# First pair of an attention-and-experts kernel: scores as three products, set-up work moved between engines and queues

## The chip, the cores and the metric

The kernel runs on one core of a Trainium2 chip. The metric is the time of one execution on the device in microseconds; less is better. Inputs and output are float32. Engines are named as in the profile: PE (TensorE matmul), PEld (its weight load), DVE (VectorE), ACT (ScalarE), POOL (GpSimd) and SP (SyncE, which only issues transfers).

## The reference, cut to what matters

Causal attention with a decay (4 batches, 8 heads, 576 positions, head dimension 64), then a routed expert layer, then a layer with a maximum of three products:

```python
scores = scale * np.matmul(q, k.transpose(0, 1, 3, 2))
cum = np.cumsum(np.log(np.clip(f, 0.0001, 1.0)), axis=-1)
scores = np.where(causal, -1e9, scores + cum[..., :, None] - cum[..., None, :])
attn = np.exp(scores - np.max(scores, axis=-1, keepdims=True))
attn = attn / (np.sum(attn, axis=-1, keepdims=True) + 1e-09)
x = np.matmul(attn, v)            # heads side by side: 2304 rows of 512
x = moe(x)                        # each row to one of 8 experts, two products
out = np.maximum(np.maximum(x @ w1, x @ w2), x @ w3) @ w_out
```

The softmax is the same when a constant is added to a row of scores, so only `-cum` of the key has to be added to the product, not that of the query.

## The kernel before, in words

**Pairs of heads.** The 32 heads are done as 16 pairs; a head's 576 queries are five tiles, taken in the order 4, 0, 3, 1, 2 (tile 0 of both heads is one product, done with the second head). For exactness each operand is split into a high part, rounded for the PE's `fp32r` mode, and a low part, the difference. Four tiles per pair, in three sets used in turn (pair `p` uses set `p % 3`): `At` holds the high part of q in its rows 0 to 63 and the low part in rows 64 to 127. `R1` holds the high part of k twice. `R2` holds the low part of k in rows 0 to 63 and, in rows 64 and 65, the decay `chi` and `clo` (high and low part of -8 times the cumulative sum). `Bt` holds the high part of q again in rows 0 to 63, copied out of `At` by a DMA, and ones in rows 64 and 65. A tile of scores is two products that accumulate in PSUM (line 377): `At` with `R1` over 128 rows, and `Bt` with `R2` over 66 rows (low k, and the decay through the ones). DVE then masks the tile and takes its maximum (line 400), ACT takes the exponential (line 424), PE transposes it (lines 439 to 447), ACT or DVE copies the transposed blocks to `PT`, PE multiplies them with V (line 506, one run of 32 products for a pair) and transposes the result back through `w144` (line 526).

**Set-up, in the order written (lines 282 to 313).** SP issues the loads of `f` and of pair 0 (q and k in halves, one half for each head). ACT's queue issues the loads of the experts' small inputs and of pair 1 (line 268). `decays` (line 74) clamps `f` (DVE), takes the logarithm (ACT), the running sum and its two parts (DVE). ACT rounds pair 0's halves to `At` and `R1` (line 297); SP copies each half of `At` to `Bt` (line 298) and brings the decay rows of pair 0 to `R2` (line 279). DVE makes the low parts of both halves (lines 303, 304). POOL fills at the very start the masks, `w144`, the ones of `Bt` in sets 1 and 2, the zero corners of the four `PT` and the last rows of the two V tiles. Then SP brings pair 1's decay rows and the first V.

**Planned part.** From line 314 on, a planner (`Sched`) writes the instructions: each task has an engine (or two to choose from), a cost, a priority and tasks it depends on; the planner keeps a modelled time per engine, starting at 9.0 for all, and always takes the task that can start first. What it fixes is each engine's order; on the chip the engines run those orders and wait for each other by semaphores. `split_tasks(p)` (line 326) makes the high parts of pair `p` on ACT or DVE, the copy to `Bt` on SP (line 349), and four low parts on POOL (lines 343, 346). `pair_out` (line 484) is the product with V and what follows. `late_rows` (line 95, the experts' normalised rows that go into `w144`) and `late_setup` (line 560) are chains of small tasks.

After attention, the experts' stage gathers rows and runs long streams of 384-column products on PE to the end.

Of the kernel before, what the change touches and what calls it, by code (L numbers as in the profile page):

```python
# [73 lines left out]
def decays(nc, g, sp):  # L74
    lf = g.lf
    chi = g.chi = sp.tile([B * H, S], F32R, name="chi")
    clo = g.clo = sp.tile([B * H, S], F32R, name="clo")
    nc.vector.tensor_scalar(out=lf, in0=lf, scalar1=1e-4, scalar2=1.0, op0=ALU.max, op1=ALU.min)
    nc.scalar.activation(out=lf, in_=lf, func=AF.Ln)
    cum = g.pp.tile([B * H, S], F32, tag="P", name="cum")  # L80
# [156 lines left out]
def attention(tc, g, qT, kT, v, x_dram, es):  # L237
# [22 lines left out]
    def zero_corners(i):  # L260
        d = PT[i][64:128, 0, 0:64]
        nc.gpsimd.memset(bass.AP(tensor=d.tensor, offset=d.offset, ap=[list(d.ap[0]), [S + 128, NBLK], [1, 64]]), 0.0)
# [14 lines left out]
    def load_decay(p):  # L277
        for r, c in enumerate((g.chi, g.clo)):
            nc.sync.dma_start(out=R2[p % NQ][64 + r:65 + r].bitcast(F32).rearrange("p r s -> p (r s)"),
                              in_=c[2 * p:2 * p + 2, :].bitcast(F32))  # L280
# [6 lines left out]
    for r in range(2):  # L287
        for t, src in ((q2, qT), (k2, kT)):
            nc.sync.dma_start(out=t[:, r], in_=src[0][:, r])
    g.mid_load()  # L290
    nc.vector.memset(g.nil, 0.0)
    nc.vector.memset(Bt[0][64:66].bitcast(F32), 1.0)
    g.decays()
    load_pair(1, nc.scalar)
    for r in range(2):
        for t, hi in ((q2, At[0]), (k2, R1[0])):
            nc.scalar.activation(out=hi[:, r], in_=t[:, r], func=AF.Copy)
        nc.sync.dma_start(out=Bt[0][0:64, r].bitcast(F32), in_=At[0][0:64, r].bitcast(F32))
        if r == 0:
            load_decay(0)  # L300
    nc.scalar.activation(out=g.nil[:, 1:2], in_=g.nil[:, 0:1], func=AF.Exp)
    for r in range(2):
        nc.vector.tensor_tensor(out=R2[0][0:64, r], in0=k2[0:64, r], in1=R1[0][0:64, r].bitcast(F32), op=ALU.subtract)
        nc.vector.tensor_tensor(out=At[0][64:128, r], in0=q2[64:128, r], in1=At[0][64:128, r].bitcast(F32), op=ALU.subtract)  # L304
    for i in range(1, NQ):
        nc.gpsimd.memset(Bt[i][64:66].bitcast(F32), 1.0)
    for i in range(NPT):
        zero_corners(i)
    for i in range(2):
        nc.gpsimd.memset(V[i][64:128, 4, :], 0.0)  # L310
# [1199 lines left out]
```

## Time and profile before

| what | us |
|---|---|
| median of 3 runs | 746.82 (745.94 to 749.03) |
| the profiled execution | 745.84 |
| its span in the trace | 744.1 |
| PE busy | 711.2 (96%) |
| DVE, ACT, POOL busy | 437.3, 375.2, 142.6 |

All times in the trace count from the start of the span. A row of the timeline gives an instruction's start, its duration, its engine and line, what it writes and reads, and in brackets how long the engine stood idle before it and what ended that. Matmuls overlap in the records, so the distance between two starts tells PE's pace, not the duration. The set-up and the first three pairs lie in the first 40 us, attention ends near 195 us, and the experts' stage fills the rest.

### The profile page before, as it was taken

To read this page: it belongs to the slowest core of one execution; us is meant where nothing else is said; L and a number is where in the kernel's file an instruction comes from. 1 tells how busy PE (TensorE), PEld (TensorE's weight loads), DVE (VectorE), ACT (ScalarE), POOL (GpSimd) and SP (SyncE) were. 2 spreads that over 40 slices of the span, in tenths; PEclk is the share of its full clock that TensorE was granted. 3 is DMA by queue.
4 is the path that set the end of the run, shared out by engine and by line. 5 is a ranking of instruction groups with operands and counts; after the bars stand their busy time and mean duration, and the time that the engine had idled before them with its cause. 6 is when DMAs were issued, how large, how long until landed. Compare 5 with 4: busy or idle time off the path is not lost. (4 is left out here: it accounts for less than half of the span.)

```text
span 744.1 us, 13151 instructions
## 1 busy us (share of the span) xinstructions
PE 711.2 (96%) x4814; PEld 671.4 (90%) x4814; DVE 437.3 (59%) x1118; ACT 375.2 (50%) x857; POOL 142.6 (19%) x140
## 2 busy tenths in 40 slices
PE   3999999999589999999999999999999999999996
PEld 2789888888489999999999999999899899998995
DVE  6788888878658887897687779512222123122220
ACT  5889899998348656546555654311211212112111
POOL 6658366440110310100210000010100100101001
PEclk9999999999869999999999999999999999999999
DMA  7768748521275665555667534000000100000001
GB/s 239 218 219 221 240 120 258 175 51 34 76 242 176 207 213 193 214 189 189 225 207 238 177 111 141 15 29 1 29 14 1 43 1 7 36 1 29 15 1 44
DMA packets 44708, 90.04 MB, mean 121 GB/s; under 512 B 23142, under 2 KB 23142, under 8 KB 44640
## 3 DMA queue, kind: packets, MB, share of 16 engines
q1 hardware_dynamic: 39984, 76.52, 32.6%
q0 software_dynamic: 3360, 9.74, 3.8%
q10 hardware_dynamic: 1296, 2.90, 1.1%
q8 instruction: 40, 0.66, 0.4%
q14 instruction: 28, 0.23, 0.1%
HBM read 74.83 MB, written 9.44 MB: 113 GB/s over the span
## 5 line engine op out<-in xcount | busy, mean ns | idle before, releaser
L1289 DVE TENSOR_TENSOR tm<-pm,tm 128x384 f32<-128x384 f32 x72 | 40.1, 557 | 178.9 <-PE pm L959 178.8
L958 PE MATMUL pm<-x_y,m 128*128 128x384 f32 x432 | 144.4, 334 | 0.0
L959 PE MATMUL pm<-x_y,m 128*128 128x384 f32 x432 | 144.4, 334 | 0.0
L957 PE MATMUL pm<-x_y,m 128*128 128x384 f32 x432 | 144.4, 334 | 0.0
L1003 DVE TENSOR_TENSOR w<-stg,w 128x1024 fp32r<-128x1024 f32 x64 | 78.0, 1223 | 22.6 <-ACT w L986 21.9
L986 ACT ACTIVATE w<-stg 128x1024 fp32r<-128x1024 f32 x62 | 65.2, 1056 | 42.4 <-DMA stg<-in_w_dram 25.7
L424 ACT ACTIVATE P<-P,nm 128x576 f32<-128x576 f32 (+2 forms) x144 | 83.8, 586 | 4.8 <-DVE nm L400 4.5
L1324 POOL DMA_INDIRECT out_dram<-oo,ctidx x18 | 17.8, 987 | 332.8 <-ACT oo L1321 329.7
L958 PEld LDWEIGHTS pm<-x_y,m 128*128 128x128 f32 x432 | 81.1, 188 | 0.3
L957 PEld LDWEIGHTS pm<-x_y,m 128*128 128x128 f32 x432 | 81.1, 188 | 0.2
L959 PEld LDWEIGHTS pm<-x_y,m 128*128 128x128 f32 x432 | 81.1, 188 | 0.0
L957 PE MATMUL ph<-x,w 128*128 128x384 f32 (+7 forms) x256 | 78.9, 308 | 0.7 <-ACT x L986 0.7
L958 PE MATMUL ph<-x,w 128*128 128x384 f32 (+7 forms) x256 | 78.8, 308 | 0.4 <-DVE novi L843 0.4
L957 PE MATMUL py<-h,w 128*128 128x384 f32 (+7 forms) x256 | 78.7, 307 | 0.0
L959 PE MATMUL ph<-x,w 128*128 128x384 f32 (+7 forms) x256 | 78.5, 307 | 0.0
L958 PE MATMUL py<-h,w 128*128 128x384 f32 (+7 forms) x256 | 77.4, 303 | 0.0
L959 PE MATMUL py<-h,w 128*128 128x384 f32 (+7 forms) x256 | 77.4, 302 | 0.0
L986 ACT ACTIVATE g<-tm 128x384 fp32r<-128x384 f32 x36 | 18.9, 524 | 111.0 <-DVE tm L1289 111.0
L377 PE MATMUL s<-R,At 128*128 128x288 f32 (+3 forms) x160 | 60.7, 384 | 9.4 <-DVE At L304 8.2
L1113 POOL DMA_INDIRECT gat<-x_dram,gidx x23 | 27.9, 1212 | 199.6 <-PE xt L1120 156.4
L400 DVE CUSTOM_DVE_ANT_0 P<-s,mask 128x288 f32<-128x288 f32 (+3 forms) x128 | 58.3, 475 | 7.7 <-PE s L377 7.0
L443 PE MATMUL t<-ident,P 128*128 128x128 f32 x320 | 57.0, 278 | 0.0
(256 smaller groups left out, 1533.3 us busy)
## 6 DMA issues: line engine op xcount, KB each, us to landing
stg<-in_w_dram SPq DMA_DIRECT2D x61, 512.0 KB
sd<-in_m_dram SPq DMA_DIRECT2D x18, 512.0 KB
q<-in_q_dram SPq DMA_DIRECT2D x14, 576.0 KB
k<-in_k_dram SPq DMA_DIRECT2D x14, 576.0 KB
Bt<-At SPq DMA_DIRECT2D x15, 288.0 KB
V<-in_v_dram SPq DMA_DIRECT2D x4, 1024.0 KB
x_dram<-XL SPq DMA_DIRECT2D x62, 64.0 KB
sd_o<-in_mo_dram SPq DMA_DIRECT2D x6, 512.0 KB
```

The lines of the kernel that those rows point to most:

```text
L377: nc.tensor.matmul(st[:, 0:wp], lt[0:kk, r, q0:q0 + 128], rt[0:kk, r, j0:j0 + wp], start=(ps_i == 0), stop=(ps_i == 1))
L400: nc.vector.tensor_tensor_reduce(out=P[0:n, j0:j0 + w], in0=st_.pop((h, t, k))[0:n, 0:w], in1=g.mask[0:n, m0:m0 + w], scale=-0.125, scalar ...
L424: nc.scalar.activation(out=P[0:n, 0:ext], in_=P[0:n, 0:ext], func=AF.Exp, bias=nm[0:n, k:k + 1], scale=-1.0, accum_out=sums[b][0:n, t, c:c ...
L443: nc.tensor.transpose(w[:, 128 * a:128 * a + 128], P[:, 128 * a:128 * a + 128], g.ident)
L957: nc.tensor.matmul(out, whi, xhi, start=start, stop=False)
L958: nc.tensor.matmul(out, whi, xlo, start=False, stop=False)
L959: nc.tensor.matmul(out, wlo, xhi, start=False, stop=stop)
L986: nc.scalar.activation(out=out, in_=in_, func=AF.Copy)
L1003: ENG[e].tensor_tensor(out=w[:, 1], in0=t, in1=w[:, 0].bitcast(F32), op=ALU.subtract)
L1113: nc.gpsimd.indirect_dma_start(out=t[0:n], out_offset=None, in_=x_dram, in_offset=bass.IndirectOffsetOnAxis(ap=idx, axis=0))
L1289: nc.vector.tensor_tensor(out=mx[0], in0=mx["p", w][:, 0:MC], in1=mx[0], op=ALU.max)
L1324: nc.gpsimd.indirect_dma_start(out=out, out_offset=bass.IndirectOffsetOnAxis(ap=g.sidx[:, col:col + 1], axis=0), in_=o[1], in_offset=None, ...
```

## The change

For pair 0 the second product takes q's high part straight from `At` (rows 0 to 63) and only low k from `R2` (64 rows); a third product adds the decay: `pick`, a tile of 64 rows in which rows r and 32+r are ones for head r and the others zero, against `cc`, which holds `chi` of all 32 heads in rows 0 to 31 and `clo` in rows 32 to 63. So pair 0 needs neither copies to `Bt` nor decay rows in `R2`. `pick` is made by POOL (a fill and two selects) and rounded by ACT. Pair 1's loads go to SP's queue right behind those of pair 0; pair 2's loads depend on pair 1's high q. The low parts of head 1 are made by POOL, those of head 0 stay on DVE. DVE gets some fills of POOL (ones of `Bt` in set 1, last rows of V 0, corners of two `PT`); POOL's other fills and `w144` become planned tasks behind the low parts of pair 1, with the experts' rows behind `w144`. `hold` is a write of the same column of `nil` by DVE and then by POOL, which makes POOL wait until DVE has come that far; it stands after the clamp and after DVE's low parts. The dummy exponential that loads ACT's table moves ahead of the last rounding. The planner's clocks start at 8.2 (PE, DVE), 8.4 (ACT) and 11.0 (POOL). The load of the second V waits for the first pair's product with V.

```diff
--- before.py
+++ after.py
@@ -71,12 +71,29 @@
                             pattern=[[0, NPAIR], [-64, 2], [-1, D]], channel_multiplier=1)
 
 
-def decays(nc, g, sp):
+def pick_rows(nc, g, sp):
+    pick = g.ones_at = sp.tile([2 * B * H, 2, 128], F32, name="ones_at")
+    g.pick = sp.tile([2 * B * H, 2, 128], F32R, name="pick")
+    nc.gpsimd.memset(pick, 0.0)
+    for c in range(2):
+        nc.gpsimd.affine_select(out=pick, in_=pick, compare_op=ALU.not_equal, fill=1.0, base=-B * H * c,
+                                pattern=[[-1, 2], [0, 128]], channel_multiplier=1)
+
+
+def hold(nc, g):
+    nc.vector.memset(g.nil[:, 2:3], 0.0)
+    nc.gpsimd.memset(g.nil[:, 2:3], 0.0)
+
+
+def decays(nc, g, sp, meanwhile):
     lf = g.lf
-    chi = g.chi = sp.tile([B * H, S], F32R, name="chi")
-    clo = g.clo = sp.tile([B * H, S], F32R, name="clo")
+    g.cc = sp.tile([2 * B * H, S], F32R, name="cc")
+    chi, clo = g.cc[0:B * H], g.cc[B * H:]
     nc.vector.tensor_scalar(out=lf, in0=lf, scalar1=1e-4, scalar2=1.0, op0=ALU.max, op1=ALU.min)
+    hold(nc, g)
+    meanwhile()
     nc.scalar.activation(out=lf, in_=lf, func=AF.Ln)
+    nc.scalar.activation(out=g.pick, in_=g.ones_at, func=AF.Copy)
     cum = g.pp.tile([B * H, S], F32, tag="P", name="cum")
     nc.vector.tensor_tensor_scan(out=cum, data0=lf, data1=g.nil[0:B * H, 0:1].to_broadcast([B * H, S]), initial=0.0,
                                  op0=ALU.add, op1=ALU.add)
@@ -257,9 +274,9 @@
     V = [fx.tile([128, NBLK, H * D], F32, name=f"V{i}") for i in range(2)]
     vt, raws, sums, XL, Pt, st_, tl_ = {}, {}, {}, {}, {}, {}, {}
 
-    def zero_corners(i):
+    def zero_corners(i, e=nc.gpsimd):
         d = PT[i][64:128, 0, 0:64]
-        nc.gpsimd.memset(bass.AP(tensor=d.tensor, offset=d.offset, ap=[list(d.ap[0]), [S + 128, NBLK], [1, 64]]), 0.0)
+        e.memset(bass.AP(tensor=d.tensor, offset=d.offset, ap=[list(d.ap[0]), [S + 128, NBLK], [1, 64]]), 0.0)
 
     def load_pair(p, eng=None):
         q2 = ld.tile([128, 2, S], F32, tag="q2", name=f"q2_{p}")
@@ -275,9 +292,10 @@
         vt[b] = t
 
     def load_decay(p):
-        for r, c in enumerate((g.chi, g.clo)):
+        for r in range(2):
+            h = B * H * r + 2 * p
             nc.sync.dma_start(out=R2[p % NQ][64 + r:65 + r].bitcast(F32).rearrange("p r s -> p (r s)"),
-                              in_=c[2 * p:2 * p + 2, :].bitcast(F32))
+                              in_=g.cc[h:h + 2, :].bitcast(F32))
 
     g.lf = pp.tile([B * H, S], F32, tag="P", name="lf")
     nc.sync.dma_start(out=g.lf, in_=g.f_in)
@@ -287,31 +305,29 @@
     for r in range(2):
         for t, src in ((q2, qT), (k2, kT)):
             nc.sync.dma_start(out=t[:, r], in_=src[0][:, r])
+    load_pair(1)
     g.mid_load()
     nc.vector.memset(g.nil, 0.0)
-    nc.vector.memset(Bt[0][64:66].bitcast(F32), 1.0)
-    g.decays()
-    load_pair(1, nc.scalar)
+    nc.vector.memset(Bt[1][64:66].bitcast(F32), 1.0)
+    nc.vector.memset(V[0][64:128, 4, :], 0.0)
+    g.decays(lambda: [zero_corners(i, nc.vector) for i in range(2)])
+    low_q = lambda e, r: e.tensor_tensor(out=At[0][64:128, r], in0=q2[64:128, r], in1=At[0][64:128, r].bitcast(F32), op=ALU.subtract)
+    low_k = lambda e, r: e.tensor_tensor(out=R2[0][0:64, r], in0=k2[0:64, r], in1=R1[0][0:64, r].bitcast(F32), op=ALU.subtract)
     for r in range(2):
-        for t, hi in ((q2, At[0]), (k2, R1[0])):
-            nc.scalar.activation(out=hi[:, r], in_=t[:, r], func=AF.Copy)
-        nc.sync.dma_start(out=Bt[0][0:64, r].bitcast(F32), in_=At[0][0:64, r].bitcast(F32))
-        if r == 0:
-            load_decay(0)
-    nc.scalar.activation(out=g.nil[:, 1:2], in_=g.nil[:, 0:1], func=AF.Exp)
-    for r in range(2):
-        nc.vector.tensor_tensor(out=R2[0][0:64, r], in0=k2[0:64, r], in1=R1[0][0:64, r].bitcast(F32), op=ALU.subtract)
-        nc.vector.tensor_tensor(out=At[0][64:128, r], in0=q2[64:128, r], in1=At[0][64:128, r].bitcast(F32), op=ALU.subtract)
-    for i in range(1, NQ):
-        nc.gpsimd.memset(Bt[i][64:66].bitcast(F32), 1.0)
-    for i in range(NPT):
-        zero_corners(i)
-    for i in range(2):
-        nc.gpsimd.memset(V[i][64:128, 4, :], 0.0)
+        nc.scalar.activation(out=At[0][:, r], in_=q2[:, r], func=AF.Copy)
+        if r == 1:
+            nc.scalar.activation(out=g.nil[:, 1:2], in_=g.nil[:, 0:1], func=AF.Exp)
+        nc.scalar.activation(out=R1[0][:, r], in_=k2[:, r], func=AF.Copy)
+    low_k(nc.vector, 0)
+    low_q(nc.vector, 0)
+    hold(nc, g)
+    low_q(nc.gpsimd, 1)
+    low_k(nc.gpsimd, 1)
     load_decay(1)
     load_v(0)
 
     sd = Sched({"s": 3, "P": NPB, "t": 2, "tl": 1, "o": 2, "ot": 2}, 9.0)
+    sd.clk.update(PE=8.2, DVE=8.2, Pool=11.0, ACT=8.4)
     act = lambda n: 0.06 + n / 1200
     dve = lambda n: 0.07 + n / 960
     pe = lambda n: 0.02 + n / 2400
@@ -321,14 +337,28 @@
     slot = {(h, t): 5 * h + i for h in range(NH) for i, t in enumerate(order)}
     side, ready, fs, fr, fe, ft, fv, ftv, fo, fb, fn_ = {}, {0: []}, {}, {}, {}, {}, {}, {}, {}, {}, {}
     vdep = {0: None}
-    rows_done = sd.chain(g.late_rows(), 8)
+
+    def fill_corners():
+        zero_corners(2)
+        zero_corners(3)
+
+    def fills():
+        late = lambda cost, prio, fn, i: sd.task("Pool", cost, lambda e: fn(), prio, ready[i])
+        late(1.0, 8, lambda: nc.gpsimd.memset(Bt[2][64:66].bitcast(F32), 1.0), 1)
+        vdep["pt"] = late(0.7, 9, fill_corners, 1)
+        base = late(1.5, 12, g.w144_base, 1)
+        vdep[1] = late(0.5, 30, lambda: nc.gpsimd.memset(V[1][64:128, 4, :], 0.0), 2)
+        late(1.05, 20, lambda: nc.gpsimd.memset(Bt[0][64:66].bitcast(F32), 1.0), 2)
+        return base
+
 
     def split_tasks(p):
         i, u = p % NQ, 10 * p - 6
-        load = None
+        load = Task(("SP",), 0.0, None, 0, [], (), 0.0)
+        load.end, load.by = 9.0, "SP"
         if p > 1:
             old = [fs[h, t, k] for h in (2 * p - 6, 2 * p - 5) for t in range(NBLK) for k in range(1 + (t == 4))] if p >= NQ else []
-            load = sd.task("SP", 0.9, lambda e: load_pair(p), u - 8, ready[p - 2], lat=4.5)
+            load = sd.task("SP", 0.9, lambda e: load_pair(p), u - 8, ready[p - 2] + ([ready[1][0]] if p == 2 else []), lat=4.5)
             dec = sd.task("SP", 1.3, lambda e: load_decay(p), u - 4, old, lat=2.0)
         else:
             old, dec = [], None
@@ -367,15 +397,20 @@
         def fn(e):
             st = st_[h, t, k] = ps_s.tile([128, 512], F32, tag="s", name=f"s_{h}_{t}_{k}")
             wp = max(w, 192)
-            for ps_i, (lt, rt, kk) in enumerate(((At[i], R1[i], 128), (Bt[i], R2[i], 66))):
+            for ps_i, (lt, rt, kk) in enumerate(((At[i], R1[i], 128), (Bt[i] if p else At[i], R2[i], 66 if p else 64))):
                 if t == 0:
                     nc.tensor.matmul(st[:, 0:192].rearrange("p (r j) -> p r j", r=2), lt[0:kk].rearrange("p r q -> p (r q)")[:, S - 64:S + 64],
                                      rt[0:kk, :, 0:96],
-                                     start=(ps_i == 0), stop=(ps_i == 1))
+                                     start=(ps_i == 0), stop=(p > 0 and ps_i == 1))
                     continue
                 q0 = ROW0[t] - (0 if r else 64)
                 nc.tensor.matmul(st[:, 0:wp], lt[0:kk, r, q0:q0 + 128],
-                                 rt[0:kk, r, j0:j0 + wp], start=(ps_i == 0), stop=(ps_i == 1))
+                                 rt[0:kk, r, j0:j0 + wp], start=(ps_i == 0), stop=(p > 0 and ps_i == 1))
+            if p == 0 and t == 0:
+                for x in range(2):
+                    nc.tensor.matmul(st[:, 96 * x:96 * x + 96], g.pick[:, x], g.cc[:, 0:96], start=False, stop=(x == 1))
+            elif p == 0:
+                nc.tensor.matmul(st[:, 0:wp], g.pick[:, r], g.cc[:, j0:j0 + wp], start=False, stop=True)
 
         fs[h, t, k] = sd.task("PE", pe(2 * max(w, 192)), fn, slot[h, t] - LEAD, side.get(h, []), get=("s", (h, t, k)))
 
@@ -507,7 +542,7 @@
                                          vt[b][:, a, (2 * hp + r) * D:(2 * hp + r + 1) * D],
                                          PT[(2 * p + r) % NPT][:, a, lo:c0 + w], start=(a == 0), stop=(a == na - 1))
 
-        fo[p] = sd.task("PE", 2.85, pv, u0 + 1, [fv[h, t] for h in hs for t in order] + [vdep[b]],
+        fo[p] = sd.task("PE", 2.85, pv, u0 + 1, [fv[h, t] for h in hs for t in order] + [vdep[b], vdep["pt"] if p == 1 else None],
                         get=[("o", ("po", p, u)) for u in range(2)], kind="tile")
         for u, (c0, w) in enumerate(RNG):
             o = {}
@@ -555,13 +590,16 @@
 
     last = [None]
     split_tasks(1)
-    consts_done = sd.chain(g.late_setup(), 25, ready[1])
+    split_tasks(2)
+    base = fills()
+    rows_done = sd.chain(g.late_rows(), 12, [base])
+    consts_done = sd.chain(g.late_setup(), 25, [base])
     for p in range(NP):
         b, hp = divmod(p, NPAIR)
-        if p + 2 < NP:
+        if 0 < p < NP - 2:
             split_tasks(p + 2)
         if hp == 1 and b + 1 < B:
-            vdep[b + 1] = sd.task("SP", 3.3, lambda e, b=b: load_v(b + 1), 40 * b + 20, [fo[NPAIR * b - 1]] if b else [], lat=2.0)
+            vdep[b + 1] = sd.task("SP", 3.3, lambda e, b=b: load_v(b + 1), 40 * b + 20, [fo[NPAIR * b - 1] if b else fo[0]], lat=2.0)
         head(2 * p)
         head(2 * p + 1)
         pair_out(p)
@@ -1453,12 +1491,12 @@
             g.qk = ea.enter_context(tc.tile_pool(name="qk", bufs=1))
             sp = ea.enter_context(tc.tile_pool(name="sp", bufs=1))
             consts(nc, g, cp, sp)
-            w144_base(nc, g, sp)
-            pair_mask(nc, g, sp)
-            g.nil = sp.tile([128, 2], F32, name="nil")
+            pick_rows(nc, g, sp)
+            g.nil = sp.tile([128, 3], F32, name="nil")
             g.f_in = f
             g.mid_load = lambda: expert_load(nc, g, emb, tau, sp)
-            g.decays = lambda: decays(nc, g, sp)
+            g.decays = lambda zeros: decays(nc, g, sp, lambda: (pair_mask(nc, g, sp), zeros()))
+            g.w144_base = lambda: w144_base(nc, g, sp)
             g.late_rows = lambda: expert_rows(nc, g, sp, g.ps_o)
             g.late_setup = lambda: routing_consts(nc, g, cp)
             g.batch_done = lambda b, X: route_batch(nc, g, b, X, rp, g.ps_o)
```

## Rows read from the trace of the kernel before

**Rows 1.** The page: its first line and PE's share of the span.

```profile
span 744.1 us, 13151 instructions
...
PE 711.2 (96%) x4814; PEld 671.4 (90%) x4814; DVE 437.3 (59%) x1118; ACT 375.2 (50%) x857; POOL 142.6 (19%) x140
```

**Rows 2.** Windows: stretch, length, busy us (instructions) per engine, PEclk, DMA share, GB/s.

```profile
0.00:10.00 10.00, 0.58 (x1) 0.29 (x1) 5.49 (x8) 4.02 (x5) 9.04 (x21) 1.00 0.76 250
...
20.00:24.00 4.00, 3.07 (x17) 2.75 (x17) 1.77 (x8) 2.00 (x7) 3.72 (x18) 1.00 1.03 309
...
40.00:60.00 20.00, 20.00 (x176) 17.27 (x176) 17.59 (x69) 17.64 (x53) 12.03 (x9) 1.00 0.68 200
...
215.00:220.00 5.00, 5.00 (x27) 5.00 (x26) 2.34 (x3) 2.35 (x3) 0.00 (x0) 0.87 0.97 339
```

**Rows 3.** PE's waits from 0 to 60 us: us in total, times, longest.

```profile
PE s L377 <- DMA Bt<-At: 4.3, 2, 3.4
...
PE pe L116 <- DVE emb L112: 0.7, 1, 0.7
```

**Rows 4.** Timeline of PE: first scores, the pace's rise, begin of the experts' stage.

```profile
8.22 0.58 PE L377 MATMUL s<-R,At 128*128 128x288 f32 x1 [8.22 <-DVE At L304]
...
12.20 0.61 PE L377 MATMUL s<-R,Bt 66*128 66x288 f32 x1 [3.40 <-DMA Bt<-At]
...
12.61 0.44 PE L377 MATMUL s<-R,At 128*128 128x288 f32 x1
...
12.85 0.44 PE L377 MATMUL s<-R,Bt 66*128 66x288 f32 x1
...
14.95 0.53 PE L377 MATMUL s<-R,At 128*128 128x192 f32 x1 [0.91 <-DVE nm L400]
...
21.74 0.30 PE L377 MATMUL s<-R,At 128*128 128x288 f32 x1
22.97 0.40 PE L377 MATMUL s<-R,Bt 66*128 66x288 f32 x1 [0.93 <-DMA Bt<-At]
23.21 0.30 PE L377 MATMUL s<-R,At 128*128 128x288 f32 x1
23.35 0.30 PE L377 MATMUL s<-R,Bt 66*128 66x288 f32 x1
...
205.11 2.34 PE L1120 MATMUL xt<-ident,gat 128*128 128x128 f32 x8 [4.07 <-DMA gat<-x_dram,gidx]
```

**Rows 5.** Timeline of the issuing queues (SPq, ACTq) in the set-up.

```profile
3.31 0.36 ACTq L268 DMA_DIRECT2D q<-in_q_dram  x1
...
4.97 0.57 SPq L298 DMA_DIRECT2D Bt<-At  x1
...
11.83 0.40 SPq L273 DMA_DIRECT2D V<-in_v_dram  x1
...
14.42 0.54 SPq L349 DMA_DIRECT2D Bt<-At  x1
```

**Rows 6.** Timeline of ACT and DVE: pair 0's high and low parts.

```profile
4.26 0.68 ACT L297 ACTIVATE At<-q 128x576 fp32r<-128x576 f32 x1 [0.28 <-DMA q<-in_q_dram]
...
7.32 0.76 DVE L304 TENSOR_TENSOR At<-q,At 64x576 fp32r<-64x576 f32 x1
...
7.96 0.69 ACT L297 ACTIVATE At<-q 128x576 fp32r<-128x576 f32 x1 [2.31 <-DMA q<-in_q_dram]
...
11.23 0.68 ACT L297 ACTIVATE R<-k 128x576 fp32r<-128x576 f32 x1 [2.58 <-DMA k<-in_k_dram]
```

**Rows 7.** Groups by line and shape, 0 to 32 us: busy us, mean ns.

```profile
L343 POOL TENSOR_TENSOR At<-q,At 64x576 fp32r<-64x576 f32 x3 | 4.2, 1411 | 0.2
...
L306 POOL MEMSET Bt<- 2x1152 f32 x2 | 2.3, 1180 | 0.0
...
L400 DVE CUSTOM_DVE_ANT_0 P<-s,mask 128x448 f32<-128x448 f32 x3 | 1.9, 617 | 1.3 <-PE s L377 1.3
...
L262 POOL MEMSET PT<- 64x320 f32 x4 | 1.3, 358 | 0.0
```

## The prediction, made before the change was run

> **What bounds the kernel now.** I read the page's first lines, then the windows, then PE's waits, then the timelines of the first 24 us. PE is busy 711.2 of 744.1 us [rows 1], and from 40 to 60 us it has no idle time at all [rows 2]: once PE has its first scores, its stream sets the end, and what is saved in front of that stream is saved at the end. So the place to look at is the set-up, where PE does 0.58 us of work in the first 10 us [rows 2]. PE's first product starts at 8.22, when DVE has the low part of q. The second one waits 3.40 us more, to 12.20, for the copy of q to `Bt` by DMA [rows 4]. That copy was issued at 4.97 [rows 5]; it had no work to do but moving 144 KB, on engines that were 0.76 busy in this stretch at 250 GB/s [rows 2]. PE waits twice for such a copy, 4.3 us in all [rows 3]; the second wait is pair 1's, 0.93 us before 22.97 [rows 4], for a copy issued at 14.42 behind V and pair 2's loads [rows 5].
>
> The pace matters too. [...] In the experts' stage PE starts at 205.11 [rows 4], and a mean of 0.87 in 215 to 220 [rows 2] puts the rise 3.7 us before 220, at 216.3: 11.2 us after the start. For the changed start I take 9.5 us, with 6.8 and 11.2 as ends.
>
> **The change, part by part.** *The start.* Head 0's three products need high q and k (ACT), both low parts (DVE) and `cc` (DVE), all done before the low q that ends at 7.32 + 0.76 = 8.1 [rows 6]. So PE goes on from its first product at 8.2 instead of 12.2. New in front of that: `pick` on POOL, a fill and two selects. Between a fill of 358 ns and one of 1180 ns each [rows 7] that is 1.1 to 3.5 us on an engine that has two masks ahead of it; I take 1.2, done near 3.5. ACT rounds it in at most the 0.68 us of a larger rounding [rows 6] before it takes q at 4.26, where it stood 0.28 us idle [rows 6]. At the low end nothing moves, at the high end the start moves 2 us; I take 0. DVE's new fills (0.36 each for two corners [rows 7], some 0.5 for V) lie in front of the clamp and beside ACT's logarithm; without that cover they would cost their 1.2 us.
>
> *The third product.* [...] The second product costs the same over 64 rows as over 66.
>
> *Adding up to the point where pair 1 begins.* Before, PE ran from 12.20 to 21.7 with one wait of 0.9 us (14.95, behind DVE's rounding of pair 1's q): 8.6 us at half pace, worth 4.3 at full. Afterwards the same work is 4.3 + 1.36 = 5.7, less the first product. From 8.2 at half pace until 17.7 PE does 4.75 of it, and the last 0.8 to 0.9 at full pace: it is there at 18.5 instead of 21.7, a gain of 3.2. With the rise at 15.0 it is there at 17.1 (4.6), at 19.4 there is no rest left (2.3).
>
> *Pair 1's wait.* Its copy to `Bt` was issued at 14.42 and landed at 22.97. Now its high q is made from loads that finish near 11 us (below), the copy is issued some 4 us earlier, and pair 2's loads stand behind it, not ahead. Needed at 18.5, behind V's 1 MB and itself: 11 + 1.3 MB at 250 GB/s = 16 to 17. So the 0.93 us go. Sum: 3.2 + 0.93 = 4.1 us. Bounds 2.3 + 0.9 = 3.2 and 4.6 + 0.9 = 5.5.
>
> *Queues.* SP loses two copies to `Bt` and two decay rows of pair 0, and gains pair 1's two loads, in front of pair 1's decay rows and V; ACT's queue loses them. Nothing of pair 0 waits behind them on SP any more. In the trace of before, pair 0's second half of q lets ACT start only at 7.96 and that of k at 11.23, after waits of 2.31 and 2.58 us [rows 6], while pair 1's loads, issued from ACT at 3.31 [rows 5], move over the same engines. Put behind them on one queue, pair 0's 1.25 MB at 250 GB/s should be there near 7 and pair 1's near 11. [...]
>
> *Head 1's low parts on POOL.* 1.41 us each against DVE's 0.76 [rows 6, 7]. They are queued behind the second `hold`, at 8.1: 8.1 + 1.41, then 1.41 behind k's rounding, with gaps 11.0 to 11.2. PE needs them after head 0's 1536 x 3 columns at half pace, 8.2 + 3.84 = 12.0. So nothing on the path; the slack is 0.8 to 1.0. What waits behind them on POOL are pair 1's four low parts: they start behind the rounding of pair 1's k, near 13, and at 1.41 with gaps of 0.1 the first two are done at 16, where PE needs them by 18.5, the others at 19. The first `hold` stops POOL until the clamp is over; behind it stands only the pair mask, which no tile needs before the second head.
>
> *Late fills and the experts' rows.* `Bt`'s ones 1.18, two corners 0.72 [rows 7] and `w144`, priced by the largest row at 1.2 to 2.4, now follow pair 1's low parts: POOL is free for pair 2 near 23, and two low parts for its first head take 3. Sixteen pairs end near 195 us, some 10 us each, so PE needs them about 10 us after 18.5: they are hidden, by 2 to 3 us. The chain of the experts' rows starts later, and PE, which waited 0.7 us for it [rows 3], may wait as long again or not at all; I leave it as it is, plus or minus 0.7. *Planner clocks* change only orders. DVE needs 0.62 us for a tile of 448 columns [rows 7], whose three products take PE 1.1 at half pace, so masking keeps up unless it stands behind a rounding that waits for data.
>
> **The number.** 745.84 (the profiled execution, span 744.1 and 1.7 around it) - 4.1 = 741.7. That execution lies 1.0 below the median of 746.82 and inside the range of the runs; for a median I say 742.0. About 0.5%, 3.7 us, is what a measurement here can tell from no change.
>
> **Rivals.**
> *The stall moves to pair 1* (chance 0.13). PE comes to pair 1 earlier, and its low parts (POOL until 16 for the first two) or its `Bt` copy are late. For it: the copy took 8.5 us from issue to use [rows 4, 5], and POOL has 2.8 us more ahead of pair 1. If pair 1's second product still starts at 22.97, the whole gain is gone: 745.8, the same. Against it: what stood ahead of that copy, pair 2's loads, is now behind it.
> *The queue doesn't order* (0.12). Then the change of queues doesn't do what it says, and pair 0's second half of k still lands at 11.2. ACT, in order, stands until 11.9; POOL's low k is done at 13.3 and PE waits 1.3 us for head 1, and ACT's first exponentials come 1 us later still: about 743.8, the same. For it: 16 engines at 0.76 whoever issues. Against it: the first halves, alone on the queue, were there at 4.26.
> *PE stays at half pace* (0.07, slower). Place: the first three heads. PE runs early but in pieces, waiting on POOL, on roundings in front of masks and on exponentials, and its pace rises only after a run without breaks. Each us at half pace costs 0.5. From a rise at 17.7 the 4.1 us are used up when the pace rises after 26; at 30 the time is 747.9, past 33 it is over 0.5% slower. For it: 11.2 us in the experts' stage, after a start in pieces. Against it: with three score buffers and 0.62 us per mask, head 0 gives an unbroken 3.8 us, and head 1 follows.
>
> **How the numbers follow.** The forecast has 0.68: of its 3.2 to 5.5 us, some 0.48 lies above 3.7 and 0.20 below. The two rivals that give most of it back add 0.25 to the same, of which I move 0.02 to faster for a part of the stall only. The slow one gives 0.05 slower and 0.02 the same. Faster 0.50, same 0.45, slower 0.05. The range starts at 742.0 - 2.7 = 739.3: the high gain, 5.5, with PE's 0.7 us of waiting gone as well, both counted against 4.1, is 2.1, and 0.6 for the spread of the runs below their median. It ends at 746.2, which takes in the moved stall at 745.8 and leaves out the slow case.
>
> **What would show it.** Right: PE's second and third products at 8.4 to 8.8 with no wait for a DMA; 11 more matmul groups on line 377 and its neighbours; ACT's second roundings near 6 and 8.5; POOL's head 1 low parts at 8.2 to 11.2; the 0.14 us pace by 17.7; pair 1's scores from 18.5 without a wait; and everything from 40 us on the same, some 4 us earlier, down to PE's first work in the experts' stage, near 201 in place of 205.11. Wrong: a wait of PE at pair 1 or for line 346 of over 1 us; ACT idle until 11; or an earlier start whose lead is smaller at 60 us than at 20, which would mean that DVE and ACT, each at 88% in 40 to 60 us [rows 2], set that stretch and not PE.

## The result and the profile after

The changed kernel takes **755.16 us**, median of 4 runs (753.97 to 755.58), against 747.15 (745.94 to 749.03) for the kernel before on the same chip: ratio 1.0102, 95% interval 1.0078 to 1.0127. It is slower by 1%; 742.0 was forecast. The profiled execution took 755.44 with a span of 753.7, against 745.84 and 744.1.

The first lines of the page of the kernel after:

```profile
span 753.7 us, 13179 instructions
...
PE 721.9 (96%) x4826; PEld 678.2 (90%) x4826; DVE 445.0 (59%) x1123; ACT 373.1 (49%) x856; POOL 144.7 (19%) x144
```

PE's share is what it was [rows 1], but it is busy 10.7 us longer (721.9 against 711.2). So PE lost little to waiting; its own work takes longer. Its waits in the first 60 us, kernel after (idle us, how often, longest):

```profile
PE s L407 <- DVE nil L84: 8.6, 1, 8.6
...
PE pe L133 <- DVE emb L129: 2.0, 1, 2.0
```

Both waits for `Bt` [rows 3] are gone, and PE starts at 8.6, 0.4 us behind the 8.2 that was forecast. A wait of 2.0 us for the experts' rows stands in the place of one of 0.7 [rows 3]. Timeline of PE, kernel after (a row with x2 holds a tile's first two products and shows the shape of the first):

```profile
8.58 1.11 PE L407 MATMUL s<-R,At 128*128 128x288 f32 x2 [8.58 <-DVE nil L84]
9.49 0.44 PE L413 MATMUL s<-cc,pick 64*128 64x288 f32 x1
9.86 1.14 PE L407 MATMUL s<-R,At 128*128 128x288 f32 x2
10.81 0.44 PE L413 MATMUL s<-cc,pick 64*128 64x288 f32 x1
11.18 1.41 PE L407 MATMUL s<-R,At 128*128 128x448 f32 x2
...
12.89 0.98 PE L407 MATMUL s<-R,At 128*128 128x192 f32 x2
...
26.97 0.59 PE L407 MATMUL s<-R,At 128*128 128x288 f32 x1
...
30.99 0.29 PE L407 MATMUL s<-R,At 128*128 128x288 f32 x1
31.12 0.30 PE L407 MATMUL s<-R,Bt 66*128 66x288 f32 x1
...
41.41 0.41 PE L133 MATMUL pe<-ident,emb 8*128 8x8 f32 x4 [2.04 <-DVE emb L129]
...
213.17 2.27 PE L1158 MATMUL xt<-ident,gat 128*128 128x128 f32 x8 [4.18 <-DMA gat<-x_dram,gidx]
```

There are three things to see. The second tile starts 1.28 us after the first (8.58 to 9.86), where three products 0.24 apart [rows 4], here called half pace, would take 0.72. Pair 1's first score comes at 26.97, 5.2 us later than the 21.74 of before [rows 4], although PE started 3.6 us before the second product of before. And the experts' stage starts at 213.17, 8.06 us behind the 205.11 of before [rows 4]. The weight loads (PEld) of the same stretch, kernel after:

```profile
9.09 0.28 PEld L407 LDWEIGHTS s<-R,At 64*128 64x128 f32 x1 [0.25 <-issue]
9.26 0.34 PEld L413 LDWEIGHTS s<-cc,pick 64*128 64x128 f32 x1
...
9.86 0.28 PEld L407 LDWEIGHTS s<-R,At 128*128 128x128 f32 x1 [0.27 <-issue]
```

The load from a 64-row tile to another 64-row tile (9.26) follows at once. The loads where the tile changes, 128 to 64 (9.09) and 64 to 128 (9.86), come after 0.25 and 0.27 us in which PEld waits for nothing that the profile shows. Windows of the kernel after (columns as in [rows 2]):

```profile
10.00:20.00 10.00, 10.00 (x26) 6.28 (x27) 4.42 (x17) 2.18 (x6) 4.75 (x5) 1.00 0.91 246
...
42.00:44.00 2.00, 1.83 (x8) 1.45 (x8) 1.95 (x10) 1.00 (x3) 1.93 (x2) 0.71 0.82 281
44.00:46.00 2.00, 2.00 (x11) 1.92 (x10) 1.40 (x7) 1.25 (x5) 1.85 (x3) 0.50 0.69 281
46.00:48.00 2.00, 2.00 (x17) 1.98 (x17) 1.30 (x6) 1.62 (x7) 1.80 (x6) 0.94 0.35 75
```

From 10 to 20 us PE is "busy" all the time and does 26 products; with 66-row tiles (e1, below) it does 45 in the same window. The wait at 41 is followed by a fall of the granted clock to 0.50 until near 46.

To compare kernels up to the end of attention I take one mark, read from one profiled execution of each: the start of PE's first product of the routing of the last batch. It is 196.93 before and 204.91 after, +7.98.

### The profile page after: what moved, and what is told of

Its sections match the earlier page's. It is cut to its first block, busy times and chain, and to the rows that moved or that the text cites. A ratio compares the mean times of both kernels' runs of the same rounds, so it can differ in the third digit from the quotient of the medians.

```text
span 753.7 us, 13179 instructions
## 1 busy us (share of the span) xinstructions
PE 721.9 (96%) x4826; PEld 678.2 (90%) x4826; DVE 445.0 (59%) x1123; ACT 373.1 (49%) x856; POOL 144.7 (19%) x144
## 5 line engine op out<-in xcount | busy, mean ns | idle before, releaser
L407 PE MATMUL s<-R,At 128*128 128x288 f32 (+6 forms) x170 | 67.9, 408 | 9.4 <-DVE nil L84 8.6
```

Of the source, the lines that this page charges most:

```text
L407: nc.tensor.matmul(st[:, 0:wp], lt[0:kk, r, q0:q0 + 128], rt[0:kk, r, j0:j0 + wp], start=(ps_i == 0), stop=(p > 0 and ps_i == 1))
```

## The experiments

Two theories followed from these lines, with a rival each. **A:** alternating 64-row and 128-row tiles is what costs; the rival is the third product itself, or the slow pace for its own sake. **B:** the late rows of the experts cost the 2 us wait and the pace behind it; the rival is that this wait is a symptom of a late start.

| kernel | time us (runs) | ratio to before, 95% | mark, us |
|---|---|---|---|
| before | 747.15 (4) | | 196.93 |
| after | 755.16 (4) | 1.0102 [1.0078, 1.0127] | 204.91 |
| e1, 66 rows | 748.53 (10) | 1.0021 [0.9998, 1.0044] | 197.82 |
| e2, 66 rows, rows in the set-up | 744.19 (10) | 0.9951 [0.9929, 0.9973] | 193.51 |
| e3, before with 64 rows | 1202.89 (1), on other data | | 254.35 |
| e4, before with three products | 748.86 (10) | 1.0017 [0.9992, 1.0042] | 195.91 |
| e5, 66 rows, rows in a gap | 743.96 (12) | 0.9934 [0.9907, 0.9961] | 193.27 |
| e6, only third product 64 rows | 752.86 (1) | | 205.43 |
| e7, 64 rows, rows in a gap | 751.24 (10) | 1.0041 [1.0021, 1.0061] | 201.74 |
| e8, e5 with 16 warm-up products | 742.75 (8) | 0.9921 [0.9889, 0.9954] | 193.74 |
| e9, e5 with 22 | 743.78 (6) | 0.9935 [0.991, 0.996] | 193.34 |
| e10, e5 with pair 1 on ACT's queue | 742.86 (4) | 0.9916 [0.9885, 0.9948] | 194.19 |

The runs e1 to e4, e5 to e8, and e9 and e10 were made on three different chips, each ratio against runs of before on the same chip (747.61, 747.78 and 749.27); between these groups the ratios and marks are to be compared, not the times.

**e1: the changed kernel with 66 rows.** Two zero rows pad `pick`, `cc` and pair 0's `R2`; all else is the change.

```diff
-    g.cc = sp.tile([2 * B * H, S], F32R, name="cc")
+    g.cc = sp.tile([2 * B * H + 2, S], F32R, name="cc")
...
+    nc.gpsimd.memset(g.cc[2 * B * H:].bitcast(F32), 0.0)
...
-            for ps_i, (lt, rt, kk) in enumerate(((At[i], R1[i], 128), (Bt[i] if p else At[i], R2[i], 66 if p else 64))):
+            for ps_i, (lt, rt, kk) in enumerate(((At[i], R1[i], 128), (Bt[i] if p else At[i], R2[i], 66))):
```

> The changed kernel, with the two 64-row products of pair 0 done over 66 rows (two rows of zeros in R2 and in pick and cc), which is the only form that the kernel before used beside 128 rows. Theory A (a change between 64-row and 128-row weight tiles keeps the next weight load from running beside the product): three products of 288 columns take 0.72 us per tile at half pace instead of 1.28, eleven tiles save about 6 us, pair 1's first scores come near 21 us instead of 27, and the time falls by 4 to 6 us, to 749 to 751. Theory B (the pace alone: PE works in pieces and stays at half pace until 29 us whatever the tiles): tiles stay above 1.2 us or the pace still rises near 29 us, and the time stays above 753. Theory C (the planner's order and the late experts' rows are the loss: a wait of 2.0 us at 41 us and a second stretch at half pace): 754 to 756, with that wait unchanged.

Two rows more, and 6.6 us less (755.16 to 748.53; 6 by the two ratios). The timeline of PE in e1:

```profile
9.53 0.68 PE L408 MATMUL s<-R,At 128*128 128x288 f32 x2
10.01 0.44 PE L414 MATMUL s<-cc,pick 66*128 66x288 f32 x1
10.25 0.95 PE L408 MATMUL s<-R,At 128*128 128x448 f32 x2
...
11.37 0.57 PE L408 MATMUL s<-R,At 128*128 128x192 f32 x2
...
20.25 0.38 PE L408 MATMUL s<-R,At 128*128 128x288 f32 x1
```

A tile of 288 columns now takes 0.72 us (9.53 to 10.25) and pair 1 begins at 20.25, 6.7 us sooner. The tile of 448 columns takes 1.12 us (10.25 to 11.37) against 1.71 after (11.18 to 12.89): the price is 0.56 and 0.59 us a tile, so it hardly grows with the columns. The windows of e1:

```profile
10.00:20.00 10.00, 10.00 (x45) 9.52 (x45) 5.41 (x23) 4.69 (x14) 7.28 (x6) 1.00 0.97 234
...
30.00:40.00 10.00, 7.65 (x46) 6.61 (x44) 8.85 (x26) 7.08 (x23) 9.57 (x7) 0.83 0.71 218
```

In 30 to 40 us PE is busy 7.65 us only: the 2 us wait for the experts' rows is still there and has come earlier. So e1 is not faster than before. Theory A holds, and B's wait is not a symptom of the late start.

**e2: e1 with `w144` made in the set-up.**

```diff
-        base = late(1.5, 12, g.w144_base, 1)
...
-    rows_done = sd.chain(g.late_rows(), 12, [base])
-    consts_done = sd.chain(g.late_setup(), 25, [base])
...
+    rows_done = sd.chain(g.late_rows(), 8)
+    consts_done = sd.chain(g.late_setup(), 25, ready[1])
...
-            g.decays = lambda zeros: decays(nc, g, sp, lambda: (pair_mask(nc, g, sp), zeros()))
+            g.decays = lambda zeros: decays(nc, g, sp, lambda: (pair_mask(nc, g, sp), zeros(), w144_base(nc, g, sp)))
```

> As the run before, and w144 filled in the set-up and the experts' rows planned from the start, as in the kernel before. Theory A alone: within 1 us of the run before. Theory C: the wait for the experts' rows near 41 us (2.0 us) and the fall of the pace after it are gone, 3 to 4 us less than the run before, 745 to 747 if A holds too, 751 to 752 if only C holds.

The mark goes from 197.82 to 193.51. B holds too, although the start moved to 9.21: `w144` is now filled beside DVE's two operations on the running sum, which take 0.74 and 1.09 us (0.45 and 0.75 after).

**e3: the kernel before with 64 rows in the second product of pairs 1 to 15**, so that only the tile changes.

```diff
-            for ps_i, (lt, rt, kk) in enumerate(((At[i], R1[i], 128), (Bt[i], R2[i], 66))):
+            for ps_i, (lt, rt, kk) in enumerate(((At[i], R1[i], 128), (Bt[i], R2[i], 64 if p else 66))):
```

> The kernel before, with the second product of pairs 1 to 15 over 64 rows instead of 66; this leaves the decay out of those pairs. Theory A: 165 tiles with two changes of weight tile each; at 0.12 us (half of the 0.25 to 0.28 seen at half pace) that is 40 us, at 0.28 it is 92, in a stretch in which PE has no idle time: 785 to 840. Without A: 746 to 748, as the columns are the same.

Without the decay the later stages work on other data, so only the attention part is read. Timeline of PE in e3, at pair 1's second product and later:

```profile
23.05 0.61 PE L377 MATMUL s<-R,Bt 64*128 64x288 f32 x1 [3.81 <-DMA Bt<-At]
...
100.87 0.38 PE L377 MATMUL s<-R,At 128*128 128x288 f32 x1
101.18 0.40 PE L377 MATMUL s<-R,Bt 64*128 64x288 f32 x1
101.50 0.66 PE L443 MATMUL t<-ident,P 128*128 128x128 f32 x4
```

With PE at full pace (products of 288 columns 0.14 apart in before [rows 4]), a tile's two products take 0.63 us (100.87 to 101.50); in the trace of before two such products of one tile, beginning at 23.21 [rows 4], are through in 0.27 where they follow scores and in 0.35 where they follow a transpose. Fifteen pairs have 165 such tiles; the mark is 57.4 us later (254.35 less 196.93), 0.35 us per tile. Some of that is pace: after the wait of 3.81 us the granted clock was 0.50 until 38 us, which costs some 7.5 us (half of the 15 from 23.05), which leaves about 0.30 us per tile (an estimate; the single tile above gives 0.28 to 0.36). So the gap needs neither the third product nor the early start, and it stands at either pace.

**e4: the kernel before with only the three products** (66 rows; no copy to `Bt`, no decay rows for pair 0). Queues, `hold`, POOL's low parts and fills stay as before.

```diff
-        nc.sync.dma_start(out=Bt[0][0:64, r].bitcast(F32), in_=At[0][0:64, r].bitcast(F32))
-        if r == 0:
-            load_decay(0)
...
-            for ps_i, (lt, rt, kk) in enumerate(((At[i], R1[i], 128), (Bt[i], R2[i], 66))):
+            for ps_i, (lt, rt, kk) in enumerate(((At[i], R1[i], 128), (Bt[i] if p else At[i], R2[i], 66))):
```

> The kernel before, with nothing of the change but the three products of pair 0 (over 66 rows, so without a change of weight tile), no copies to Bt and no decay rows for pair 0. The prediction's own steps (start 3.7 to 4 us earlier, third product 1.4 to 2.7): 742 to 745. Theory B: no gain, 746 to 748, since the pace rises later. If it gives the gain and the first run doesn't, what is lost lies in the moved fills, loads and orders.

This missed: 748.86, no gain, and a mark only 1.0 us earlier. Pair 1's first scores come at 20.28, but its second product waits 0.58 us for its decay rows at 21.16, and pair 0's product with V starts at 28.20, where e5 has it at 24.43. PE does not wait for V there; it waits 0.55 us for a mask, 0.58 for the decay rows and 0.67 for the experts' rows, and the product with V stands later in its order. So the early start alone is not enough. How the rest of the missing gain divides between these waits and the order was not taken apart. The ACT timeline of e4 shows something else:

```profile
6.38 0.68 ACT L310 ACTIVATE At<-q 128x576 fp32r<-128x576 f32 x1 [0.46 <-DMA q<-in_q_dram]
7.10 0.68 ACT L310 ACTIVATE R<-k 128x576 fp32r<-128x576 f32 x1
```

Pair 0's second halves come at 6.38 and 7.10 instead of 7.96 and 11.23 [rows 6], with pair 1's loads still on ACT's queue.

**e5: e1 with `w144` behind pair 0's last low part on POOL**, ahead of pair 1's.

```diff
     low_k(nc.gpsimd, 1)
+    g.w144_base()
...
-        base = late(1.5, 12, g.w144_base, 1)
...
-    rows_done = sd.chain(g.late_rows(), 12, [base])
-    consts_done = sd.chain(g.late_setup(), 25, [base])
...
+    rows_done = sd.chain(g.late_rows(), 8)
+    consts_done = sd.chain(g.late_setup(), 25, ready[1])
```

> The first run's kernel (66 rows), with w144 filled by POOL right behind head 1's low parts, where POOL stands idle for 5 us, and the experts' rows planned from the start. If the late rows were what e1 lost to e2: PE's wait for the experts' rows and the second stretch at half pace are gone as in e2, and as w144 no longer lies beside the running sum, PE starts near 8.6 us instead of 9.2: 743 to 745, equal to e2 or 0.5 us less. If what e2 gained came from its other order by chance: 746 to 749.

743.96 against 747.78 for before beside it, faster by 0.4 to 0.9%. The window of e5 to hold against e1's 7.65:

```profile
30.00:40.00 10.00, 10.00 (x88) 8.47 (x86) 8.58 (x35) 8.84 (x23) 8.02 (x8) 1.00 0.80 235
```

**e6: the changed kernel with 64 rows in the third product only** (the second has 66, on zero rows as in e1).

```diff
-            for ps_i, (lt, rt, kk) in enumerate(((At[i], R1[i], 128), (Bt[i] if p else At[i], R2[i], 66 if p else 64))):
+            for ps_i, (lt, rt, kk) in enumerate(((At[i], R1[i], 128), (Bt[i] if p else At[i], R2[i], 66))):
```

> The changed kernel with the second product of pair 0 over 66 rows and only the third over 64. Theory A1 (the cost is per change of tile size; there are two changes per tile as before): tiles of 288 columns still 1.2 to 1.3 us apart, time 753 to 756. Theory A2 (each 64-row product costs by itself): half of the excess, tiles near 1.0 us apart, time 750 to 753.

Timeline of PE in e6:

```profile
8.53 0.82 PE L407 MATMUL s<-R,At 128*128 128x288 f32 x2 [8.53 <-DVE nil L84]
9.27 0.61 PE L413 MATMUL s<-cc,pick 64*128 64x288 f32 x1
9.81 0.85 PE L407 MATMUL s<-R,At 128*128 128x288 f32 x2
10.59 0.61 PE L413 MATMUL s<-cc,pick 64*128 64x288 f32 x1
11.12 1.11 PE L407 MATMUL s<-R,At 128*128 128x448 f32 x2
```

One 64-row product instead of two, and a tile still takes 1.28 to 1.31 us (8.53, 9.81, 11.12); the mark is 205.43, as late as after. The price goes by the number of changes, two per tile, not by the number of 64-row products. The single time of 752.86 lies where the other theory had it, but the trace shows each tile, and I go by that.

**e7: the changed kernel with its 64 rows, `w144` placed as in e5** (the same lines).

> The changed kernel with its 64-row products, and only the experts' rows planned from the start and w144 filled behind head 1's low parts. If the two losses add up, this gives back the 4 us that e2 gained on e1 and keeps the 6 to 7 us of the tile changes: 750 to 752. If the late rows mattered only because PE came early, there is nothing to gain here: 754 to 756.

The mark is 201.74, between after and e5: placing the rows gains 3.2 us here (204.91 to 201.74) and 4.6 at 66 rows (197.82 to 193.27). With the rows in place the tiles cost 8.5 (201.74 less 193.27), with the rows late 7.1. So the two losses overlap, but by 1.4 us only.

**e8 and e9: PE warmed up before the start.** 16 products of zeros ahead of the first score; in e9 22 of them, with `Bt[1]`'s ones moved from DVE to POOL.

```diff
+    warm = R1[2][:, 0, 0:448]
+    nc.vector.memset(warm.bitcast(F32), 0.0)
+    wo = ps_o.tile([128, 512], F32, tag="o", name="warm_o")
+    for i in range(16):
+        nc.tensor.matmul(wo[:, 0:448], warm[:, 0:128], warm, start=True, stop=True)
```

> As the first run of this set, with 16 products of 448 columns of zeros on PE from about 1.5 us on, into a buffer that nobody reads, while PE has nothing else to do. If the pace rises with what PE did before, whatever it computed: 288-column products stand 0.14 us apart well before 18 us, and up to half of the 9 to 10 us at half pace comes back: 739.5 to 742. If PE is not the bound there (ACT, DVE and POOL are), PE only waits more and the time is that of the first run of this set within 1 us.

> As the run with 16 products of zeros, with 22 of them, so that PE has no 1.6 us of idle time between the last of them and the first scores, and with the ones of Bt in set 1 moved from DVE to POOL's gap, so that DVE isn't later for the zeros. If the fall of the pace at 10 us in that run came from the idle time before it: 288-column products stand 0.14 us apart all the way, the first scores of pair 1 come at 15 to 17 us instead of 20, and the time is 739 to 742. If the pace falls again although PE has no idle time, or if pair 1's data (POOL's low parts from 12 to 18 us) is what PE then waits for: 742.5 to 744.5.

Neither differs from e5 by more than the runs scatter; the gain hoped for (739 to 742) did not come. Timeline of PE in e8, and one window of it:

```profile
1.49 5.90 PE L316 MATMUL warm_o<-R 128*128 128x448 f32 x16 [1.49 <-DVE R L313]
9.01 0.51 PE L412 MATMUL s<-R,At 128*128 128x288 f32 x2 [1.61 <-DVE nil L84]
...
9.48 0.43 PE L412 MATMUL s<-R,At 128*128 128x288 f32 x2
...
12.21 0.68 PE L412 MATMUL s<-R,At 128*128 128x288 f32 x2
```

```profile
10.00:20.00 10.00, 10.00 (x44) 9.47 (x43) 6.01 (x25) 5.83 (x16) 8.95 (x8) 0.51 0.87 261
```

Two products take 0.43 us at 9.48 and 0.68 at 12.21: the pace had risen, and fell again near 10.2, after PE had been idle 1.6 us between the last warm-up product and the first score; the granted clock was 0.51 in 10 to 20 us. In e9, with no idle stretch before the first score, the full pace lasts from 9.1 to about 20.7, and the clock is 0.50 from 21 to 24. That the idle time made the difference is likely, not shown: e9 also has six products more. Timeline of PE in e9:

```profile
18.00 0.40 PE L412 MATMUL s<-R,At 128*128 128x288 f32 x1 [1.12 <-POOL At L378]
...
19.10 0.37 PE L412 MATMUL s<-R,Bt 66*128 66x288 f32 x1 [0.70 <-DMA Bt<-At]
```

PE is there at 18.0, and now waits for pair 1: 1.12 us for POOL's low part and 0.70 for the copy to `Bt`. The mark is 193.34, e5's is 193.27. At this point pair 1's data is the bound, and a faster start is worth nothing more.

**e10: e5 with pair 1's loads back on ACT's queue.**

```diff
-    load_pair(1)
...
     g.decays(lambda: [zero_corners(i, nc.vector) for i in range(2)] + [nc.gpsimd.memset(R2[0][64:66].bitcast(F32), 0.0)])
+    load_pair(1, nc.scalar)
```

> As the run with w144 in POOL's gap (66 rows), with pair 1's loads issued from ACT's queue as in the kernel before instead of behind pair 0's on SP's. If the order on one queue is what brought pair 0's second halves early: they let ACT start near 8 and 11 us again, head 1's low k is done near 13.3, PE waits 1 us or so, and the time is 1 to 2 us more, 745 to 746. If the move of queue is worth nothing: within 0.7 us, 743.3 to 744.7.

This missed both ranges, on the side of the second: 742.86, no slower (the ratio is 0.9916 against 0.9934 for e5, and the intervals overlap). The mark is 0.9 us later than e5's. Timeline of ACT in e10:

```profile
5.96 0.68 ACT L318 ACTIVATE At<-q 128x576 fp32r<-128x576 f32 x1
...
8.07 0.67 ACT L321 ACTIVATE R<-k 128x576 fp32r<-128x576 f32 x1
```

The second halves are there all the same. In e4 and e10 pair 1 is on ACT's queue, pair 0's copies and decay rows are gone, and the halves are early. So pair 1's new place is not needed for it. What brings them forward is most likely the going of those transfers; it is not shown, as pair 1's loads are also issued some 0.4 us later there (3.69 and 3.72 against 3.31 [rows 5]), and copies and decay rows were not tried apart.

## Why the prediction was wrong

**The step that failed** is one sentence: "The second product costs the same over 64 rows as over 66." I looked at columns and durations, and the trace of before had no 64-row tile beside a 128-row one, so it had no row for the change of tile; I set it at zero without bounds. It costs 0.56 us per tile at half pace (1.28 less 0.72), twice 0.28. Eleven tiles of pair 0 make 6.2 us (an estimate). By e1 the whole of it is 7.09 us at the mark (204.91 less 197.82); the remaining 0.9 I have not taken apart. Between 128 and 66 rows the products stand 0.24 apart (e1); between 128 and 64 rows PEld is idle 0.25 and 0.27 us ahead of the loads at the two changes (9.09 and 9.86 in after). Why the loads come later there no run shows.

**The second term mis-sized** is the experts' rows, set at "plus or minus 0.7". POOL, DVE in the kernel after, where the rows are made:

```profile
36.23 0.58 POOL L121 TENSOR_TENSOR ess<-ess 8x1 f32<-8x1 f32 x1
36.80 1.41 POOL L376 TENSOR_TENSOR R<-k,R 64x576 fp32r<-64x576 f32 x1
38.28 1.80 POOL L373 TENSOR_TENSOR At<-q,At 64x576 fp32r<-64x576 f32 x1
```

```profile
32.42 0.75 DVE L515 CAST R<-k 128x1152 fp32r<-128x1152 f32 x1
...
36.86 1.97 DVE L515 CAST At<-q 128x1152 fp32r<-128x1152 f32 x1
38.75 0.14 DVE L123 RECIPROCAL ess<-ess 8x1 f32<-8x1 f32 x1
38.93 1.17 DVE L124 SCALAR_TENSOR_TENSOR ess<-ess 8x1 f32<-8x1 f32 x1
```

With `w144` behind pair 1's low parts, the rows' operation on POOL (36.23) stands among pair 2's low parts, the next DVE operation of the chain comes at 38.75 behind a rounding, and PE, in order, stands before 41.41. The rounding and the operation at 38.93 take 3.14 us together, beside POOL's subtractions, and 0.96 without (0.75 above and 0.21 in before). By this estimate of 2.2 us, the wait comes as much from where the chain fell as from its being late. I had checked that the *fills* were hidden, and not what stands behind them in a chain that PE waits for. The wait is 2.04 us; by e1 and e5, which differ in this alone but for the planner's place of the routing constants, its place costs 4.55 (197.82 less 193.27): the wait, and the half pace behind it that e1's and after's windows show.

**The sum.** At the mark: all else in the change, the start above all, -3.66 (e5 against before), late rows +4.55, tile changes +7.09, together +7.98. The sum closes by construction, as e5, e1 and after differ by one step each; with the steps in the other order (e7) the rows cost 3.17 and the tiles 8.47. The 9.6 us between the two profiled executions is 1.6 more; after has one wait of 1.7 us in the experts' stage which before has not. Such waits come to 0 to 2.8 us in the profiled executions of these kernels, with the instructions of that stage in the same order, so I do not put it down to the change.

**What was right.** The start works as the prediction has it, and with the two faults taken away the total is near: -4.1 forecast, -3.66 in e5. That it is so near is partly luck. At pair 1's first score e5 leads by 1.71 us (21.74 [rows 4] against 20.03), where 3.2 was forecast; the 0.93 of pair 1's copy is gained as forecast; and PE's wait of 0.7 for the experts' rows [rows 3], which the forecast left in, is gone in e5. The 0.3 that remain lie in the order of the work and were not taken apart. The 9.5 and 6.8 us from start to rise lie between 12.20 and 14.95 and the product at 21.74, 0.30 us long against 0.44 at 12.61 [rows 4]. No run shows the 1.36 us that the sum takes for the third product: from the start of each to that of the next product, the eleven take 1.78 us in e9, at full pace, and 2.90 in e5, nearly all at half. That 8.6 us at half pace are worth 4.3 at full fits the granted clock of 0.50 (44 to 46 in after); by the 0.24 and 0.14 us of 288 columns they are 5.0 (an estimate). PE goes on without a DMA at 8.6; the pace rises 10 us after the start in e5 (18.5 to 18.7; 17.7 forecast), and pair 1 begins at 20.03 instead of 18.5. Timeline of PE in e5:

```profile
20.03 0.38 PE L407 MATMUL s<-R,At 128*128 128x288 f32 x1
```

ACT's second roundings, kernel after:

```profile
5.78 0.68 ACT L317 ACTIVATE At<-q 128x576 fp32r<-128x576 f32 x1 [0.19 <-DMA q<-in_q_dram]
...
7.88 0.67 ACT L320 ACTIVATE R<-k 128x576 fp32r<-128x576 f32 x1
```

They are near the 6 and 8.5 that were forecast, but the reason given (pair 1 behind on one queue) is not supported: e10 moves the queue back and they stay. `pick`, `hold` and the zero fills cost at most the 0.4 us by which 8.58 lies behind the 8.2 of the forecast, and PE did not wait for POOL's head 1 (in e9, at full pace, it does, 0.40 us).

**The rivals.** "PE stays at half pace" had the right sign and place, and the wrong mechanism. The pace did rise late, at 28.9. By its own price (0.5 us for each us past 26) that is worth 1.5 us, 747.3 in all, not 755; and e9 shows that a faster pair 0 is worth next to nothing with the tiles at 66 rows. With 66 rows and the same start the pace rises 10 us sooner, so the late rise came with the gaps; it adds to their price (the part of the 7.09 beyond 6.2, perhaps), but is not the first cause. "The queue doesn't order" had it right that the move of queue is not what brings the halves, as e10 shows, and its result wrong: the halves were early all the same. Whether a queue keeps its order no run shows. "The stall moves to pair 1" did not happen here, but it is the next bound: e9 meets it. The range missed because its slow end took in only costs that the trace of before could show; an operation in a form without a row was given no upper bound.

## What to carry to other kernels

When an edit gives a product another number of rows, look for a row with that tile size beside its neighbours' size; if there is none, put a price on every change of size, or pad with zero rows to a size that is already there (66 rows in place of 64 gained 6.6 us here). When a fill is moved later, follow not the fill but the chain behind it to the engine that sets the end, in the order of every queue it passes. Both losses hide a real gain: with them out (e5), the change is 0.4 to 0.9% faster than before.

## What the runs showed of the hardware

- Products on a 64-row tile between products on 128-row tiles cost a gap at each change: together 0.54 to 0.60 us for the two changes of a tile, for tiles of 192 to 448 columns, at half pace (after against e1; 288 columns 0.24 us apart there), and about 0.3 us at full pace (e3, 0.63 us for two products of 288 columns; 0.27 and 0.35 in before). A 66-row tile had no such gap (products 0.24 apart in e1, 0.14 in before).
- PE read as 100% busy in these gaps (window 10 to 20 of after); only the count of products (26 against 45 in e1) and PEld's busy time (6.28 against 9.52 us) told.
- The full pace came 10 to 11 us after the first score in e1 (8.67 to 19.2) and e5 (8.69 to 18.6), and 20 us after it in after (8.58 to 28.9), where the start has gaps; the granted clock read 1.00 in after's window of 10 to 20 us all the same. In e8, after 5.9 us of products and 1.6 us of idle time, the pace was full at 9.48, fell near 10.2 and came back near 20.
- Beside POOL's subtractions some operations of DVE in after were longer and others not: a rounding of 1152 columns took 1.97 us instead of 0.75, an operation on one column 1.17 instead of the 0.21 of before, and one of POOL's own 1.80 instead of 1.41. The masks of 448 columns took 0.62 with or without POOL beside them.
